# Loading q and k of two token blocks at once in a fused sliding-window attention and MLP kernel

## The chip, the cores and the metric

The kernel runs on one core of one Trainium2 chip. The metric is the time of one execution on the device in microseconds (us), smaller is better. A core has five engines that run their own instruction streams and meet through semaphores: PE (TensorE, matrix multiply and transpose), DVE (VectorE), ACT (ScalarE), POOL (GpSimd) and SP (SyncE, which here only issues transfers). Transfers between the chip's memory and the core are carried by 16 DMA engines, whichever engine issues them.

## The reference, cut to what matters

Eight sequences of 576 tokens pass through attention with 8 heads of 64 and a window of 128 tokens with a bias linear in the distance; the heads are joined to rows of 512, and each row goes through a layer norm and a two-layer MLP (512 to 2048 to 512) with a residual.

```python
scores = scale * np.matmul(q, k.transpose(0, 1, 3, 2))        # q, k, v: [8, 8, 576, 64] f32
mask = (rel >= 0) & (rel < window)                            # window = 128
scores = np.where(mask, scores + bias[None], -1000000000.0)
attn = softmax(scores)                                        # written out in the original
x = np.matmul(attn, v)                                        # then [8, 576, 512]
xn = (x - mu) / np.sqrt(var + 1e-06) * g_ln
out = x + np.maximum(xn @ w_ch1, 0.0) @ w_ch2
```

## The kernel before, in words

**Tiling.** The 8 × 576 = 4608 tokens form 36 blocks of 128. Two sequences are nine blocks (a "pair"); the fifth block of each pair holds the last 64 tokens of one sequence and the first 64 of the next, so its loads are split in two (`where`, L316). A block needs keys and values of itself and of the block before it. For the MLP the blocks are joined to ten chunks of 2, 3, 4, 3, 4, 4, 4, 4, 4, 4 blocks (L229).

**One block of attention** (`attention`, L412). SP loads q, k and v in f32, one token per partition, 8 runs of 64 numbers each (L329). q and k are cast to f16 (L427, `cq` and `ck`), v too (L440, `cv`). For blocks 0 to 11 PE turns q and k with eight 128×128 transposes into one bank of PSUM (L450, task `T`), and one copy of 1024 numbers per partition takes them to the tile `qkt` (L458 or L460, `ev`); for blocks 12 to 35 a transposing DMA does this (L465). PE multiplies q and k (L485, `S`) into a pair of score banks `sc`, of which there is only one set. In blocks 0 to 5 PE first lays the bias into those banks (L500, `Z`), in the others a mask is multiplied in after the exponential (L531, `mka` and `mkb`, one for each half of the heads). ACT takes the exponential (L524), PE multiplies with v (L548), and DVE normalises (L564, L568), takes the statistics (L585, L590) and forms the centred and scaled row `xs` (L596), for which it needs `g_t`, the layer norm's factor spread over all partitions. `xs` is turned by PE (L608, `TX`, with a copy at L616 or L618) for blocks 0 to 13, by a DMA (L623) from there on.

**One chunk of the MLP** (`mlp`, L645): for each of 16 slices of the hidden layer four matmuls (L657, phase A) and a relu (L667 or L669); then for each block 16 matmuls (L683, phase B), the residual (L691) and a store (L699). The weights come in eight transfers that POOL issues and that cast to f16 on the way (L404 for the first matrix, `w0` to `w3`; L406 for the second, `w4` to `w7`). Slice f of phase A needs transfer f // 4. `W_AFTER` (L393) says behind which cast each is issued: 3 × block + 0, 1, 2 for the casts of q, k, v.

**The order of the work.** Nothing is scheduled by the compiler. `Plan.run` (L88) simulates the engines and queues with a duration for each task, takes on each engine the ready task with the smallest value `v`, and gives out every instruction in the order so found; so each engine's order is fixed when the kernel is built, and an engine stands still when the next instruction in its order is not ready. A task of attention has a value that puts it `LEAD` × `SPAN` = 52 us of planned time ahead of the MLP of the same block (L311). A task with several engines in its cost goes where the plan says it ends first; `PICK` (L258) overrides the default engine for single tasks. The plan's transfers share the engines by `rates` (L82): while POOL's queue moves, SP's is planned at 0.17 of full speed. Rings of tiles (L285 to L301) set how far each loader may run ahead: five tiles each of `q32` and `k32`, four of `qk16` and `qkt`.

**Before 26 us of planned time** (`WARM`, L257) PE's planned gaps are filled with matmuls on a tile of zeros (`keep_warm`, L710, L712), which keeps its clock up and computes nothing of the result.

The lines that set the order:

```python
    def av(i, stage=0.0):
        return (i / CB - LEAD) * SPAN + stage
    W_AFTER = [8, 14, 15, 15, 16, 17, 17, 18]
            return {q: 0.92 if q == "DMA POOL" else 0.17 / (len(on) - 1) for q in on}
```

Of the kernel before, what the change touches and what calls it, by code (L numbers as in the profile page):

```python
# [46 lines left out]
class Plan:  # L47
# [6 lines left out]
    QUEUE_ROOM = 4.0  # L54
    LANDING = 2.0

# [18 lines left out]
    def transfer(self, name, eng, issue, secs, room, emit, deps=(), v=0.0):  # L75

        i = self.add(name + ".i", (eng, issue), emit, deps, v, lat=0.0)
        d = self.add(name, ("DMA " + eng, secs), None, [i], v, lat=self.LANDING)
        i.room = d.room = room
        return i, d  # L80

    def rates(self, queues):  # L82
        on = [q for q, x in queues.items() if x]
        if "DMA POOL" in on and len(on) > 1:
            return {q: 0.92 if q == "DMA POOL" else 0.17 / (len(on) - 1) for q in on}
        return {q: 1.0 / len(on) for q in on}

    def run(self):  # L88
# [7 lines left out]
        queues = {e: [] for e in sorted({e for t in self.tasks for e in t.eng if e.startswith("DMA")})}  # L96
        free = dict.fromkeys(engines, 0.0)
        avail = {e: [] for e in engines}
# [6 lines left out]
        for t in self.tasks:  # L105
            if t.left == 0:
                heap.append((0.0, n, t))
                n += 1
# [6 lines left out]
        def done(t):  # L115
            nonlocal n
            for u in t.users:
                u.ready = max(u.ready, t.end + t.lat)
                u.left -= 1
                if u.left == 0:  # L120
                    heapq.heappush(heap, (u.ready, n, u))
                    n += 1
# [7 lines left out]
        while left:  # L130
# [60 lines left out]
            for q in rate:  # L191
                if queues[q][0][1] <= 1e-9:
                    t = queues[q].pop(0)[0]
                    t.end = now
                    used[q] -= t.room
                    self.order.append((t, q, None))
                    left -= 1
                    done(t)
# [5 lines left out]
def kernel(  # L204
# [10 lines left out]
    nc = tc.nc  # L215
# [41 lines left out]
    WARM = 26.0  # L257
    PICK = {('xt', 0): 'ACT DVE', ('xt', 8): 'ACT DVE', ('cv', 5): 'ACT', ('cv', 0): 'POOL ACT', ('ev', 8): 'DVE ACT', ('ev', 1): 'ACT', ('mkb', 8): 'POOL', ('mkb', 3): 'POOL', ('mka', 2): 'DVE', ('mkb', 4): 'POOL'}  # L258
    G_AT = 1.3
    BY_BIAS = 6  # L260
    MASK_AT = 6
    QK_BY_DMA = 12
    X_BY_DMA = 14

    plan = Plan()

    def sb(name, shape, dt):
# [16 lines left out]

    q32 = ring("q32", 5, [P, H, D], FP32)  # L285
    k32 = ring("k32", 5, [P, H, D], FP32)
    v32 = ring("v32", 5, [P, H, D], FP32)
    qk16 = ring("qk16", 4, [P, 2, d_model], FP16)
    vx = ring("vx", 5, [P, H, VD], FP16)
    qkt = ring("qkt", 4, [P, 2, HP, P], FP16)  # L290
    probs = ring("probs", 3, [P, 4, 2, 2 * P], FP16)
# [8 lines left out]
    rstd = ring("rstd", 4, [P, CB], FP32)  # L300
    rec = ring("rec", 4, [P, 4], FP32)  # L301

    scs = [psum.tile([P, 2, 512], FP32, tag=f"sc{n}", name=f"sc{n}") for n in range(2)]
# [20 lines left out]

    def load(name, src, r, i, v):
        got = []
        for p0, n, b, s0 in where(i):
            def emit(e, bank, p0=p0, n=n, b=b, s0=s0):
                nc.sync.dma_start(  # L329
                    out=r[i][p0 : p0 + n, :, :],  # L330
                    in_=src[b, :, s0 : s0 + n, :].rearrange("h p d -> p h d"),
                )
            t, d = plan.transfer(f"{name}{i}", "SP", 0.6, 1.22 * n / P, n / P, emit, (), v)
            r.writes(i, t)
            got.append(d)
        return got

    setup = []
    nc.scalar.preload_act_table_set("natural_log_exp_and_others")
    nc.vector.memset(warm_t, 0.0)  # L340
    nc.vector.memset(eps_t, eps)
    for t in vx.tiles:
        nc.vector.memset(t[:, :, D:VD], 1.0)

    d_iden = plan.transfer("iden", "ACT", 0.5, 0.15, 0.0, lambda e, b: nc.scalar.dma_start(out=iden, in_=iden_dram.ap()), (), -1e6)[1]
    d_dist = plan.transfer("dist", "ACT", 0.5, 0.45, 0.0, lambda e, b: nc.scalar.dma_start(out=dist_t, in_=dist_dram.ap()), (), -9e5)[1]
    d_g = plan.transfer(
        "g", "SP", 0.6, 1.3, 0.12,
        lambda e, b: nc.sync.dma_start(out=g_t, in_=moe_g_ln.unsqueeze(0).broadcast_to([P, d_model])), (), av(G_AT) - 300,  # L349
    )[1]  # L350

# [7 lines left out]
    for bank in range(4):  # L359
        for slot in range(2):  # L360
            def emit(e, b, bank=bank, slot=slot):
                nc.scalar.activation(
                    out=mreg[:, bank, slot, :], in_=dist_t[:, 0, :], func=AF.Exp,
                    scale=-float(slopes[head_of(bank, slot)]),
                )
            tm.append(add(f"mreg{bank}{slot}", ("ACT", 0.4), emit, [d_dist], av(MASK_AT, -10.0)))
    tmix, tnew = [], []
# [15 lines left out]

    loads, kept = {}, {}
    for i in range(NBLK):
        vl = av(i) - 300
        loads[i] = (
            load("q", q, q32, i, vl),
            load("k", k, k32, i, vl + 0.01),
            load("v", v, v32, i, vl + 0.02),  # L390
        )

    W_AFTER = [8, 14, 15, 15, 16, 17, 17, 18]  # L393
    t_w = {}

    def weights(i, casts):

        for n, at in enumerate(W_AFTER):
# [9 lines left out]
            t_w[n] = plan.transfer(f"w{n}", "POOL", 0.8, 3.2, 0.0, emit, [casts[at % 3]] + last, av(i, -60.0))  # L408

    qkt_done, vx_done, aggr_done, xs_done, xt_done = {}, {}, {}, {}, {}  # L410

    def attention(i):  # L412
# [7 lines left out]
        def e_cast(a, src):  # L420
            def emit(e, b):
                en = {"POOL": nc.gpsimd, "DVE": nc.vector}.get(e)
                s = src[i][:, :, :].rearrange("p h d -> p (h d)")
                if en is None:
                    nc.scalar.activation(out=qk16[i][:, a, :], in_=s, func=AF.Copy)
                else:
                    en.tensor_copy(out=qk16[i][:, a, :], in_=s)  # L427
            return emit

        def pick(name, default, **cost):  # L430
            return {e: cost[e] for e in PICK.get((name, i), default).split()}
        cq = add(f"cq{i}", pick("cq", "POOL", POOL=0.62, ACT=0.6, DVE=0.35), e_cast(0, q32), lq, av(i, 0.0))
        ck = add(f"ck{i}", pick("ck", "POOL", POOL=0.62, ACT=0.6, DVE=0.35), e_cast(1, k32), lk, av(i, 0.1))
        q32.reads(i, cq); k32.reads(i, ck); qk16.writes(i, cq); qk16.writes(i, ck)

# [6 lines left out]
        v32.reads(i, cv); vx.writes(i, cv)  # L442
        weights(i, (cq, ck, cv))

        if i < QK_BY_DMA:
            def e_t(e, b):
                pt = fb[b][:, :].bitcast(FP16).rearrange("p (a hp c) -> p a hp c", a=2, hp=HP)
                for a in range(2):
                    for hp in range(HP):
                        nc.tensor.transpose(pt[:, a, hp, :], qk16[i][:, a, hp * P : hp * P + P], iden[:, :])  # L450
            tt = add(f"T{i}", ("PE", 0.48), e_t, [cq, ck, d_iden], av(i, 1.0), acq=("fb", f"T{i}"))
            qk16.reads(i, tt)

            def e_ev(e, b):
                src = fb[plan.held[f"T{i}"][1]][:, :].bitcast(FP16)
                dst = qkt[i][:, :, :, :].rearrange("p a hp c -> p (a hp c)")
                if e == "DVE":
                    nc.vector.tensor_copy(out=dst, in_=src)  # L458
                else:
                    nc.scalar.activation(out=dst, in_=src, func=AF.Copy)  # L460
            ev = add(f"ev{i}", pick("ev", "DVE", DVE=0.7, ACT=1.02), e_ev, [tt], av(i, 1.2), rel=f"T{i}")
            qkt.writes(i, ev)
        else:
            def e_td(e, b):
                nc.sync.dma_start_transpose(  # L465
                    out=qkt[i][:, :, :, :].rearrange("p a hp c -> p (a hp) c"),
                    in_=qk16[i][:, :, :].rearrange("p a d -> p (a d)"),
                )
            ti, ev = plan.transfer(f"QT{i}", "SP", 1.4, 1.4, 1.0, e_td, [cq, ck], av(i, -4.0))
            qk16.reads(i, ev)  # L470
            qkt.writes(i, ti)
        qkt_done[i] = ev

        prev = [] if r == 0 else [qkt_done[i - 1]]

# [32 lines left out]
        if bias:  # L508
            z_ = [add(f"Z{i}", ("PE", 0.87 if r else 0.46), e_z, t_sid + [d_dist], av(i, 1.5), acq=("sc", f"S{i}"))]
        else:  # L510
            z_ = []
        s_ = add(f"S{i}", ("PE", 0.64 if r else 0.42), e_s, z_ + [ev] + prev, av(i, 2.0), acq=("sc", f"S{i}"))
        qkt.reads(i, s_)
# [200 lines left out]
    with tc.manual_schedule():  # L714
        busy = 0.9
        for t, e, b in order:
# [36 lines left out]
```

## Time and profile before

| | us |
|---|---|
| median of 7 executions | 331.96 (330.15 to 333.29) |
| the profiled execution: time | 330.3 |
| its span, from the first to the last event in the trace | 328.5 |
| PE idle between 38.4 and 324.6 us | 2.3 of 286.1 |
| last landing of v's second part for block 4, as its cast shows it | 26.9 |
| first matmul of phase A | 24.9 |

The profile is one execution recorded by the hardware. Its row for an engine and a line gives the number of instructions, their busy time and the mean of one; matmuls overlap, so a busy PE need not be at its peak, and 16 matmuls with 128 columns of output take less than 16 times the duration of one. The chain of waits follows the last instruction back to whatever released it, step by step. A table of windows gives the busy time of every engine in stretches of the span, with the share of time in which the 16 DMA engines held a packet (it passes 1 where packets overlap) and the rate at which bytes moved.

In the first 200 us of 328.5 the DMA engines are busy all the time; 150,704 of the 159,696 packets are under 512 bytes, since a row of one head is 64 × 4 = 256 bytes. The store of an output block moves packets of 2 KB. The granted clock of PE is 0.998 over the span.

### The profile page before, as it was taken

What the parts mean: (1) busy time and instruction counts of PE and PEld (TensorE: products, weight loads), DVE (VectorE), ACT (ScalarE), POOL (GpSimd) and SP (SyncE); (2) the same over time, 40 slices, a digit from 0 to 9 for tenths busy, and PEclk for the clock granted to TensorE, in tenths of its full rate; (3) what the DMA queues carried; (4) which work ended last, traced back from release to release, by engine and by line L of the source; (5) the groups of instructions that cost most, each with busy time, mean ns of one, the idle gap of its engine ahead of it and who ended that gap; (6) DMA issues with size and microseconds to landing.
All of it is one profiled execution on the core that took longest, in us unless ns stands there. A gap on an engine that the chain in (4) does not pass through costs nothing.

```text
span 328.5 us, 6816 instructions
## 1 busy us (share of the span) xinstructions
PE 318.4 (97%) x2701; PEld 175.4 (53%) x2701; DVE 182.6 (56%) x402; ACT 155.0 (47%) x249; POOL 80.8 (25%) x126
## 2 busy tenths in 40 slices
PE   8998899989999999899999999999999999999995
PEld 8987665655544565444554544444455444444442
DVE  1488714799801299844885566656556755511011
ACT  5445554534740582557336722772277227405600
POOL 3848102585300233123322422412000000000000
PEclk9999999999999999999999999999999999999999
DMA  9999999999999999999999999624323220011011
GB/s 184 210 194 193 203 195 210 228 199 235 265 218 219 264 197 165 213 255 213 193 203 228 192 204 261 134 48 116 99 49 76 90 86 21 20 64 64 2 64 64
DMA packets 159696, 52.06 MB, mean 158 GB/s; under 512 B 150704, under 2 KB 154928, under 8 KB 159664
## 3 DMA queue, kind: packets, MB, share of 16 engines
q1 hardware_dynamic: 155152, 47.20, 72.6%
q0 software_dynamic: 4224, 4.19, 7.7%
q8 instruction: 21, 0.34, 0.5%
q10 hardware_dynamic: 288, 0.23, 0.2%
q14 instruction: 11, 0.09, 0.1%
HBM read 37.19 MB, written 9.44 MB: 142 GB/s over the span
## 4 chain that ended last, share of the span: by engine, by line
PE 84%; SPq 6%; DMA 5%; DVE 3%; issue 1%; POOL 0%; ACT 0%; POOLq 0%
PE fb L657 37%; PE fb L683 37%; SPq L329 5%; PE sc L485 5%; PE fb L548 4%; DMA w1sb<-in_moe_w_ch_dram 3%; DMA v<-in_v_dram 2%; PE fb L608 1%; DVE ot L691 1%; DVE xs L596 1%; DVE probs L531 0%; DVE xb L568 0%; PE fb L450 0%; DVE st L585 0%; SPq L349 0%
## 5 line engine op out<-in xcount | busy, mean ns | idle before, releaser
L657 PE MATMUL fb<-xt,w1sb 128*128 128x512 f16 (+2 forms) x640 | 134.0, 358 | 2.1 <-DMA w1sb<-in_moe_w_ch_dram 1.9
L683 PE MATMUL fb<-w2sb,ht 128*128 128x512 f16 x576 | 132.3, 379 | 0.1
L669 ACT ACTIVATE ht<-fb 128x512 f16<-128x512 f32 (+2 forms) x143 | 79.9, 560 | 91.6 <-PE fb L657 89.2
L657 PEld LDWEIGHTS <-w1sb 128*128 128x128 f16 x640 | 59.5, 98 | 57.9 <-DMA w1sb<-in_moe_w_ch_dram 2.5
L524 ACT ACTIVATE probs<-sc 128x1024 f16<-128x1024 f32 (+1 forms) x72 | 67.4, 973 | 44.4 <-PE sc L485 44.3
L683 PEld LDWEIGHTS <-ht 128*128 128x128 f16 x576 | 53.6, 98 | 59.4 <-issue 0.2
L691 DVE SCALAR_TENSOR_TENSOR ot<-fb,rstd,xb 128x512 f32<-128x512 f32 x36 | 26.9, 748 | 60.8 <-PE fb L683 58.2
L531 DVE TENSOR_TENSOR probs<-probs,mreg 128x1024 f16<-128x1024 f16 (+1 forms) x47 | 31.1, 666 | 25.7 <-ACT probs L524 25.5
L440 POOL CAST vx<-v 128x512 f16<-128x512 f32 x34 | 21.4, 634 | 87.3 <-PE fb L548 60.0
L427 POOL CAST qk<-q 128x512 f16<-128x512 f32 x36 | 23.5, 654 | 66.9 <-DMA qkt<-qk 50.1
L568 DVE TENSOR_TENSOR xb<-fb,rec 128x256 f16<-128x256 f32 x72 | 30.0, 421 | 2.1
L548 PEld LDWEIGHTS <-probs 128*128 128x128 f16 x544 | 23.6, 97 | 13.4 <-DVE probs L531 3.4
L596 DVE SCALAR_TENSOR_TENSOR xs<-xb,mv,g_t 128x512 f16<-128x512 f16 x36 | 29.1, 807 | 1.1
L548 PE MATMUL fb<-vx,probs 128*128 128x65 f16 x544 | 26.6, 193 | 1.4 <-DVE probs L531 1.1
L427 POOL CAST qk<-k 128x512 f16<-128x512 f32 x36 | 23.6, 655 | 14.6 <-DMA k<-in_k_dram 6.4
L585 DVE BATCH_NORM_STATS2 st<-xb 128x6 f32<-128x512 f16 x36 | 24.9, 690 | 0.8
L564 DVE RECIPROCAL rec<-fb 128x4 f32<-128x4 f32 x72 | 12.7, 177 | 17.5 <-PE fb L548 17.0
L485 PEld LDWEIGHTS <-qkt 64*128 64x128 f16 x544 | 15.4, 94 | 11.1 <-issue 10.2
L485 PE MATMUL sc<-qkt 64*128 64x128 f16 x288 | 19.4, 216 | 0.0
L485 PE MATMUL sc<-qkt,qkt 64*128 64x128 f16 x256 | 18.1, 219 | 0.4 <-DVE qkt L458 0.3
L712 PE MATMUL fb<-warm_t 128*128 128x128 f16 x197 | 15.8, 241 | 1.0 <-DVE warm_t L340 1.0
L458 DVE COPY qkt<-fb 128x1024 f16<-128x1024 f16 x11 | 7.5, 679 | 13.6 <-PE fb L450 6.9
(35 smaller groups left out, 105.5 us busy)
## 6 DMA issues: line engine op xcount, KB each, us to landing
out_dram<-ot SPq DMA_DIRECT2D x36, 256.0 KB, 2.8
q<-in_q_dram SPq DMA_DIRECT2D x32, 256.0 KB, 5.0
k<-in_k_dram SPq DMA_DIRECT2D x32, 256.0 KB, 4.9
v<-in_v_dram SPq DMA_DIRECT2D x32, 256.0 KB, 4.6
w1sb<-in_moe_w_ch_dram POOLq DMA_DIRECT2D x4, 512.0 KB, 8.0
w2sb<-in_moe_w_ch_dram POOLq DMA_DIRECT2D x4, 512.0 KB, 16.1
q<-in_q_dram SPq DMA_DIRECT2D x8, 128.0 KB, 5.0
k<-in_k_dram SPq DMA_DIRECT2D x8, 128.0 KB, 4.5
```

The source lines that it names most:

```text
L427: en.tensor_copy(out=qk16[i][:, a, :], in_=s)
L485: nc.tensor.matmul(scs[half][:, g, c0 : c0 + P], kt[rows, 1, hp, :], qkt[i][rows, 0, hp, :], start=not bias, stop=True, skip_group_check=True,
L524: nc.scalar.activation(out=o, in_=n_, func=AF.Exp, scale=inv_sqrt_d)
L531: en.tensor_tensor(out=pv, in0=pv, in1=mask[:, 2 * half : 2 * half + 2, :, lo:], op=ALU.mult)
L548: nc.tensor.matmul(pp[:, hh * (D + 1) : hh * (D + 1) + D + 1], probs[i][:, bank, slot, side * P : side * P + P], vx[i - 1 + side][:, h, 0 ...
L568: nc.vector.tensor_tensor(out=xb[i][:, 256 * half : 256 * half + 256].rearrange("p (h d) -> p h d", d=D), in0=pp[:, :, 0:D], in1=rec[2 * i ...
L585: nc.vector.bn_stats(out=st[i][:, :], in_=xb[i][:, :])
L596: nc.vector.scalar_tensor_tensor(out=xs[i][:, :], in0=xb[i][:, :], scalar=mv[c][:, j, 0:1], in1=g_t[:, :], op0=ALU.subtract, op1=ALU.mult,)
L657: nc.tensor.matmul(fb[b][:, 0:n_], w1sb[:, kb, f * P : f * P + P], xt[c][:, kb, 0:n_], start=(kb == 0), stop=(kb == NKB - 1),)
L669: nc.scalar.activation(out=ht[c][:, f, 0:n_], in_=src, func=AF.Relu)
L683: nc.tensor.matmul(pm[:, :], ht[c][:, f, j * P : j * P + P], w2sb[:, f, :], start=(f == 0), stop=(f == NFB - 1),)
L691: nc.vector.scalar_tensor_tensor(out=ot[i][:, :], in0=fb[plan.held[key][1]][:, :], scalar=rstd[c][:, j : j + 1], in1=xb[i][:, :], op0=ALU. ...
```

## The change

**The loads.** In the first pair of sequences, blocks 0 and 1, 2 and 3, 5 and 6, 7 and 8 form four spans of 256 tokens. q and k of a span are loaded in one transfer each, 512 KB, with tokens 2p and 2p+1 on partition p, so that a run is 512 bytes (`load_span`, tiles `qs` and `ks`). Block 4 and the blocks from 9 on load as before. One cast of 1024 numbers per partition for q and one for k puts even tokens before odd ones (`qs16`, `ks16`). PE turns q of both blocks into one bank and k of both into another, eight transposes each; each bank is then copied out in two parts, one for each block, that write every second column, so that the tokens stand in order in `qkt`. v is loaded as before.

**Beside it:** `g_t` is no longer loaded by SP as 128 copies of a row; one row is loaded on ACT's queue and spread by a matmul with a row of ones and a copy (`G`, `Gc`). The distance table comes in two transfers. `W_AFTER` puts w1, w2 and w3 behind the v cast of block 4, w4 behind that of block 5, and w5 to w7 behind that of block 6. PE turns q and k up to block 12 (`QK_BY_DMA` 13) and `xs` up to block 10 (`X_BY_DMA` 11). `q32` and `k32` have four tiles instead of five, `qkt` five instead of four. The plan has other landing times, a later begin, and a reserve of 0.1 us (0.4 us after 30 us of plan, 0.5 us behind POOL's transfers) before PE uses what another engine made. `PICK` is longer: among what it now says, both mask products of block 6 go to POOL (`mka`, `mkb`), that of block 8 goes back from POOL to DVE, and of the two-part copies three are on ACT, one on either.

```diff
@@ class Plan
-    LANDING = 2.0
+    BEGIN = 0.75
+    LANDING = {"DMA SP": (0.7, 1.3), "DMA ACT": (0.7, 1.3), "DMA POOL": (1.6, 1.4)}
+    LAST_OF_RUN = 1.0
...
-            return {q: 0.92 if q == "DMA POOL" else 0.17 / (len(on) - 1) for q in on}
+            a, b = (0.92, 0.17) if len(queues["DMA POOL"]) > 1 else (0.7, 0.4)
+            return {q: a if q == "DMA POOL" else b / (len(on) - 1) for q in on}
...
-                u.ready = max(u.ready, t.end + t.lat)
+                late = self.slack(t, t.end) if "PE" in u.eng and "PE" not in t.eng else 0.0
+                u.ready = max(u.ready, t.end + t.lat + late)
@@ constants
+    SPANS = [0, 2, 5, 7]
+    SLACK = (0.1, 0.4, 0.5)
-    QK_BY_DMA = 12
-    X_BY_DMA = 14
+    QK_BY_DMA = 13
+    X_BY_DMA = 11
-    q32 = ring("q32", 5, [P, H, D], FP32)
-    k32 = ring("k32", 5, [P, H, D], FP32)
+    q32 = ring("q32", 4, [P, H, D], FP32)
+    k32 = ring("k32", 4, [P, H, D], FP32)
-    qkt = ring("qkt", 4, [P, 2, HP, P], FP16)
+    qkt = ring("qkt", 5, [P, 2, HP, P], FP16)
+    qs = ring("qs", 2, [P, H, 2 * D], FP32)
+    ks = ring("ks", 2, [P, H, 2 * D], FP32)
+    qs16 = ring("qs16", 2, [P, 2, H, D], FP16)
+    ks16 = ring("ks16", 2, [P, 2, H, D], FP16)
@@ g
+    d_row = plan.transfer("g", "ACT", 0.5, 0.02, 0.0, lambda e, b: nc.scalar.dma_start(out=g_row[:, :], in_=moe_g_ln.unsqueeze(0)), (), -8e5)[1]
+    def e_g(e, b):
+        nc.tensor.matmul(fb[b][:, :], one_t[:, :], g_row[:, :], start=True, stop=True)
...
+    t_g = add("G", ("PE", 1.3), e_g, [d_row], av(0, 4.0), acq=("fb", "G"))
+    d_g = add("Gc", {"ACT": 0.6, "DVE": 0.69}, e_gc, [t_g], av(0, 4.5), rel="G")
@@ loads
+    def load_span(name, src, r, n, i, v):
+        (_, _, b, s0), = where(i)
+        def emit(e, bank):
+            nc.sync.dma_start(
+                out=r[n][:, :, :],
+                in_=src[b, :, s0 : s0 + 2 * P, :].rearrange("h (p t) d -> p h (t d)", t=2),
+            )
+        t, d = plan.transfer(f"{name}{i}", "SP", 0.6, 1.75, 1.0, emit, (), v)
...
-    W_AFTER = [8, 14, 15, 15, 16, 17, 17, 18]
+    W_AFTER = [8, 14, 14, 14, 17, 18, 18, 20]
...
-        weights(i, (cq, ck, cv))
+        weights(i, (cv, cv, cv) if i in span_of else (cq, ck, cv))
@@ attention, the first block of a span
+                for a, r_, w_ in ((0, qs, qs16), (1, ks, ks16)):
...
+                        dst = w_[n][:, :, :, :]
+                        src = r_[n][:, :, :].rearrange("p h (t d) -> p t h d", t=2)
...
+                    cs = add(f"c{key}", pick(f"cs{a}", "POOL", POOL=1.25, ACT=1.02), e_c, [span_load[n][a]], av(i, 0.1 * a))
...
+                        for hp in range(HP):
+                            for t in range(2):
+                                nc.tensor.transpose(
+                                    pt[:, hp, t, :], w_[n][:, t, 2 * hp : 2 * hp + 2, :].rearrange("p h d -> p (h d)"), iden[:, :]
+                                )
+                    tt = add(key, ("PE", 0.48), e_t, [cs, d_iden], av(i, 1.0 + 0.01 * a), acq=("fb", key))
...
+                    for blk in range(2):
+                            src = fb[plan.held[key][1]][:, :].bitcast(FP16).rearrange("p (hp t c) -> p hp t c", hp=HP, t=2)[
+                                :, :, :, HALF * blk : HALF * blk + HALF
+                            ]
+                            dst = qkt[i + blk][:, a, :, :].rearrange("p hp (c t) -> p hp t c", t=2)
...
+                        ev = add(f"e{key}{blk}", pick(f"ev{a}{blk}", "DVE ACT", DVE=0.6, ACT=0.6), e_ev, [tt], av(i + blk, 1.2), rel=key)
```

## The prediction

> **What bounds the kernel now.** I read the chain of waits first, in order of time:
>
> ```profile
> 19.53 0.74 SPq L329
> 20.32 6.43 DMA v<-in_v_dram
> 26.87 0.61 POOL vx L440
> 27.66 0.50 issue
> 28.17 0.55 POOL qk L427
> 28.72 9.67 DMA w1sb<-in_moe_w_ch_dram
> 38.44 2.57 PE fb L657 x20
> ```
>
> Everything before these lines is SP issuing loads (L329, and L349 for g_t). So the chain is: fifteen loads until v of block 4 has landed, its cast, the q cast of block 5, the weight transfer w2 behind it, and from 38.44 us PE. Then the windows before and after that point, and the groups of PE up to it:
>
> ```profile
> 24.90:38.40 13.50, 11.26 (x160) 8.97 (x160) 11.72 (x32) 7.09 (x12) 6.72 (x10) 1.00 1.22 196
> 38.44:324.56 286.12, 283.85 (x2176) 144.79 (x2176) 158.22 (x330) 136.06 (x217) 59.87 (x92) 1.00 0.77 154
> L712 PE MATMUL fb<-warm_t 128*128 128x128 f16 x197 | 15.8, 241 | 1.0 <-DVE warm_t L340 1.0
> ```
>
> Second and third number of a window: its length, and PE's busy time. After 38.44 PE idles 2.3 of 286 us: there it is the bound, and little can be won. Before it, PE runs 197 matmuls on zeros, about 0.06 us apart (a run of 20 spans 1.12 us of weight loads), so 11.8 us, and idles 2.2 us in the second window. This is what an earlier supply can turn into work: when the loads and weights come x us sooner, PE is saturated x us sooner and the rest follows. That the first 38 us wait for bytes and not for an engine is in the last two columns of the windows (DMA share, GB/s):
>
> ```profile
> 10.00:15.00 5.00, 5.00 (x93) 4.48 (x87) 3.13 (x8) 2.16 (x4) 3.70 (x7) 1.00 1.19 215
> 60.00:80.00 20.00, 18.96 (x205) 11.16 (x203) 17.93 (x39) 9.81 (x15) 13.54 (x17) 1.00 1.20 205
> 298.00:324.00 26.00, 26.00 (x122) 11.79 (x121) 1.80 (x3) 9.35 (x16) 0.00 (x0) 1.00 0.10 36
> ```
>
> **Loads.** Between 10 and 15 us there are only 256-byte packets: 215 GB/s over 16 engines is 13.4 GB/s each, 19 ns a packet, 1.22 us for a 256 KB load (64 packets per engine). No 512-byte packet exists in this trace. The near row on the other side is the 2 KB packet of the stores: 26 us × 16 × 0.10 = 41.6 us of engine time for 36 GB/s × 26 us = 0.94 MB, 457 packets, 91 ns each. On the line between the two, 512 bytes take 19 + 256 × 72 / 1792 = 29 ns, so a span load takes 64 × 29 ns = 1.88 us where two loads took 2.44: 0.56 us less. The ends: 1.22 us (a packet costs the same whatever its size) and 2.44 us (bytes alone count). A rule speaks for less: the Trainium skill, DMA: Bandwidth & Descriptors, section "Why small descriptors are slow (HBM only)", charges a packet its 32-byte beats plus 3 cycles, 11 for 256 bytes and 19 for 512, so 2.44 × 19/22 = 2.11 us, 0.33 less. I take the line between the rows, because the rule gives a 2 KB packet 67 beats, 6.1 times a small one, and the rows say 91/19 = 4.8. Up to v of block 4 there are four span loads: **−2.3 us** by the rows, −1.3 by the rule, 0 to −4.9 by the ends. The four span loads after it come behind that point and are not counted.
>
> g_t was 128 packets of 2 KB on the same queue ahead of block 2's loads: 8 per engine × 91 ns, **−0.7 us**. Its substitute is hidden: one matmul in place of zeros, one copy of about 0.7 us while DVE is busy 1.84 of the first 10 us; g_t is first read at 13.4 us, and a row on ACT's idle queue lands in about 2 us, as iden did (1.9). Uncovered it would cost that copy. The later two thirds of the distance table are wanted only by block 4, and their 0.5 us issue stands before no exponential that is late.
>
> **Weights.** w1 was issued at 27.43, w2 at 28.72, since block 5's q cast lay between; an issue takes 0.75. Back to back, w2 gains **−0.5 us**, and the loads of block 5 no longer come before it. Sum for w2's landing: 38.44 − 3.5 = 34.9. What is late next? Z, S and the exponentials share one set of score banks: 22.22 (Z of block 3) to 25.68 (its exponentials' end), 3.8 us a block with the hand-over. With block 0 at about 10.3 (one longer load and cast: its q landed at 3.96 and k at 5.77, now some 0.7 and 1.3 later), S of block 4 can be at 25, where it was at 29.39; so these banks do not bind. Block 5's span, two loads of 512 KB, now queues behind w1 to w3 and comes at some 38 to 41 us where S of block 5 ran at 33.04. Its 2.4 us of PE work move back; phase A of chunks 0 and 1, for which w0 to w3 are there, covers it.
>
> **PE's own work.** Transposes of q and k: eight per block as before, plus block 12: +0.45 us (the chain has eight L450 at 0.45); three blocks' TX fewer, 4 each, 0.22 us: −0.66. **−0.2 us.** DVE loses three copies of 0.42 and gains one of 0.68. One DMA transpose of q and k goes, three of xs come; SP's queue is far from the end there.
>
> **Copies out of PSUM.**
>
> ```profile
> L458 DVE COPY qkt<-fb 128x1024 f16<-128x1024 f16 x11 | 7.5, 679 | 13.6 <-PE fb L450 6.9 <-ACT ht L669 6.7
> L616 DVE COPY xt<-fb 128x512 f16<-128x512 f16 x12 | 5.1, 422 | 5.5 <-PE fb L608 5.4
> L531 POOL TENSOR_TENSOR probs<-probs,mreg 128x1024 f16<-128x1024 f16 x1 | 2.5, 2487 | 1.8 <-ACT probs L524 1.8
> 68.27 1.95 DVE L596 SCALAR_TENSOR_TENSOR xs<-xb,mv,g_t 128x512 f16<-128x512 f16 x1
> ```
>
> The first two rows: 512 more numbers cost 257 ns,[...] over 165 ns of fixed cost. The new copies write every second number. Here a rule speaks against the change: the Trainium skill, VectorE: DVE Perf Modes, section "Mode 2×_1P", asks for a step of one for two f16 per cycle. By the rows at full rate a half copy costs 0.42, by the rule 0.165 + 512 × 1.04 ns = 0.70 us. I take 0.70. Of 16 half copies three are on ACT and one on either, where the nearest row (L618, 512 numbers) is 0.59; 12.5 on DVE are 8.8 us against 4.8 for seven whole ones, so +4 us of DVE (+0.4 at full rate), half of it before 25 us and half at 40 to 60. The cover: DVE is busy 6.9 of 20 us at 40 to 60, but 18.1 of 22 at 18 to 40. **+0.5 us**, between 0 and 2 if none of the first half is covered. The casts of 1024 on POOL are two of 0.61 in one, no loss but the wait for the whole.
>
> **Masks.** The third and fourth row: a mask product takes 2.49 us on POOL, where the plan counts 1.4; while it ran (67.17 to 69.66), xs on DVE took 1.95 instead of 0.75, and PE idled 1.0 us for it (the 60 to 80 window). This one returns to DVE: **−1.0 us**. Both of block 6 go to POOL: their second half ends 2 × 1.09 = 2.2 us after plan, less the 0.4 of reserve, 1.8. PE's order is fixed and L548 of block 6 stands before MLP matmuls that are ready. How many stand between is not in the trace, so half: **+0.9 us**, from 0 to what rival D says.
>
> **Sum:** −2.3 − 0.7 − 0.5 − 0.2 − 1.0 + 0.5 + 0.9 = −3.3 us. The profiled execution took 330.3 (span 328.5 and 1.8 around it): 327.0. It lies 1.7 below the median of the runs shown; moved to that, 331.96 − 3.3 = **328.7 us**. About 0.5% (1.7 us) is what a measurement of this kernel tells from no change.
>
> **Rivals.**
> - **C, packets cost the same whatever their size.** Then four span loads save 4.9 instead of 2.3: 326.1. For it: DMA share above 1 with small packets, so something other than the bytes fills the engines. Against: 2 KB packets do take longer.
> - **B, the transfer is hidden anyway.** Bytes bind, or the weight transfers, spaced by their own bytes (phase A goes on at 33.60 with w1 and at 38.44 with w2, 4.8 us apart), bind from w0 on. The span loads give nothing: 328.7 + 2.3 = 331.0. For it: 6.4 us from issue to landing of w0 beside the loads. Against: w1 itself waits for block 4's v.
> - **D, POOL's masks of block 6 become the bound.** Two of 2.49 us one behind the other, and DVE held behind each, by 1.2 us as seen or by all of 2.49; mean 1.85. With 2.2 us after plan: 2.2 + 2 × 1.85 = 5.9 in place of 0.9: **333.7**. It decides the sign from 4.2 us of standstill at block 6 (3.3 + 0.9). For it: the 1.0 us that one such product already cost. Against: at 40 to 60 DVE has room and PE has phase A and B of two chunks.
>
> **Chances.** Forecast 0.50 (327.2 to 330.2: the ends of copies, weights and the rule for the loads), C 0.18, B 0.16, D 0.16. The range takes in C with half a microsecond and B, and of D the lighter part: 325.6 to 332.8. Faster by over 0.5% (below 330.3): forecast, C and a little of B, 0.69. Slower by over 0.5% (above 333.6): D from its middle on, and what I may have missed in a new fixed order of every engine, 0.15. Within: 0.16.
>
> **What would show it.** Loads: span loads 1.9 us apart while they follow each other, over 240 GB/s before 15 us; v of block 4 cast near 24 instead of 26.87. Weights: first L657 near 22.5 instead of 24.89, the last wait for a weight at 35. Fewer L712, by about 50. Copies: half copies on DVE at 0.70. Masks: L531 on POOL twice at 2.5 and an idle PE before L548 of block 6. The prediction is wrong if v of block 4 lands no earlier, or if PE's idle time after its saturation grows from 2.3 us to over 5.

## The result, and the profile after

The changed kernel takes **327.5 us** (median of 12 executions, 326.6 to 329.9) where the kernel before takes 332.2. The medians differ by 4.6 us; the ratio over all executions, which is used from here on, is 0.9873, 95% interval 0.9848 to 0.9898, so 4.2 us less, between 3.4 and 5.0. The forecast was 3.3 us less. Executions more than 1.5% above the fastest of their kernel are left out of every ratio as slow: ten of 22 for the kernel without spans, its profiled one among them, and at most three for any other. The profiled execution took 327.1 (span 325.3), 3.2 us under that of the kernel before.

The chain of waits of the changed kernel, in order of time (start, length, what):

```profile
9.44 7.90 DMA v<-in_v_dram
...
20.25 10.76 DMA v<-in_v_dram
...
32.49 6.77 issue
39.31 2.12 POOL probs L636
...
42.20 2.14 POOL probs L636
...
44.39 0.42 PE fb L653 x8
44.81 2.39 PE fb L762 x16
```

It no longer ends its first part in a wait for a weight. It runs through two v loads, through 6.8 us in which POOL had nothing to do (it waited for ACT's exponentials), and from 39.3 us through the mask products of block 6 on POOL (lines have moved: L762 is phase A, L788 phase B, L653 the product with v, L636 the mask, L817 the matmuls on zeros).

Windows of the changed kernel (columns: length, then busy time of PE, PEld, DVE, ACT, POOL, granted clock, DMA share, GB/s):

```profile
5.00:10.00 5.00, 5.00 (x61) 4.03 (x59) 0.69 (x1) 4.17 (x11) 2.84 (x4) 1.00 1.23 260
10.00:15.00 5.00, 4.94 (x88) 4.47 (x87) 1.02 (x4) 3.96 (x8) 4.35 (x5) 1.00 1.17 250
15.00:20.00 5.00, 4.39 (x89) 3.89 (x83) 3.93 (x10) 3.85 (x6) 3.22 (x5) 1.00 0.74 161
20.00:30.00 10.00, 7.57 (x133) 6.61 (x127) 7.21 (x16) 5.33 (x8) 7.29 (x10) 1.00 1.15 226
30.00:40.00 10.00, 10.00 (x156) 8.72 (x154) 8.65 (x24) 9.12 (x17) 1.99 (x3) 1.00 1.20 223
40.00:60.00 20.00, 19.45 (x167) 11.56 (x165) 9.65 (x19) 12.37 (x24) 11.04 (x11) 1.00 1.15 219
60.00:80.00 20.00, 20.00 (x185) 11.28 (x184) 17.04 (x40) 7.75 (x13) 9.63 (x15) 1.00 1.04 231
80.00:140.00 60.00, 60.00 (x496) 31.94 (x494) 36.82 (x76) 30.27 (x49) 13.97 (x22) 1.00 1.15 209
```

The same for the stretches before and after 40 us, first of the kernel before, then of the changed one, and the zeros of the changed one (columns of the last line: busy time, mean ns of one, idle time before them):

```profile
0.00:40.00 40.00, 36.13 (x540) 31.98 (x541) 24.23 (x72) 19.79 (x35) 21.81 (x36) 1.00 1.16 197
40.00:140.00 100.00, 97.76 (x851) 54.38 (x849) 61.11 (x130) 48.67 (x81) 32.28 (x48) 1.00 1.16 217
```

```profile
0.00:40.00 40.00, 35.90 (x543) 31.73 (x544) 22.77 (x69) 27.72 (x46) 19.90 (x29) 1.00 1.06 217
40.00:140.00 100.00, 99.45 (x845) 54.78 (x842) 63.51 (x134) 50.39 (x85) 34.63 (x47) 1.00 1.13 215
L817 PE MATMUL fb<-warm_t 128*128 128x128 f16 x176 | 13.9, 244 | 1.0 <-DVE warm_t L363 1.0
```

**Where the time came from.** Over the whole span PE's busy time falls from 318.4 to 316.6 us and its idle time from 10.1 to 8.7. The 21 matmuls on zeros that are gone make some 1.3 us of the busy time (0.06 us each). The idle time has moved: before 40 us it is 4.1 us where it was 3.9, from 40 to 140 it is 0.55 where it was 2.2, and after 140 it is the same 4.0. So PE is full from 30 us on, not from 38.4; but 1.7 of the 3.2 us between the two profiles come from idle time after 40 us, where the prediction saw little to win. PE is not fed as predicted either. The timeline of POOL and PE in the changed kernel:

```profile
18.45 0.88 POOL L466 DMA_DIRECT2D w1sb<-in_moe_w_ch_dram  x1
21.36 0.61 POOL L504 CAST vx<-v 128x512 f16<-128x512 f32 x1
22.80 0.75 POOL L466 DMA_DIRECT2D w1sb<-in_moe_w_ch_dram  x1
26.13 1.27 POOL L520 CAST qs<-qs 128x1024 f16<-128x1024 f32 x1 [2.58 <-DMA qs<-in_q_dram]
27.35 1.48 POOL L466 DMA_DIRECT2D w1sb<-in_moe_w_ch_dram  x2
...
27.46 0.62 PE L530 MATMUL fb<-iden,qs 128*128 128x128 f16 x8 [1.59 <-POOL qs L520]
...
30.57 1.92 PE L762 MATMUL fb<-xt,w1sb 128*128 128x256 f16 x16
```

v of block 4 is cast at 21.36 us where it was 26.87, and w1 is issued at 22.80 where it was 27.43. That is 5.5 us, and the prediction had 2.9 (near 24). The two loads of this v now go out ahead of the first weight transfer, w0, at 18.45; in the kernel before they went out behind it. First the kernel before, then the changed one:

```profile
18.42 0.93 POOL L404 DMA_DIRECT2D w1sb<-in_moe_w_ch_dram  x1
19.53 1.62 SPq L329 DMA_DIRECT2D v<-in_v_dram  x2
```

```profile
16.41 1.31 SPq L352 DMA_DIRECT2D v<-in_v_dram  x2
```

The second of the two took 6.4 us from its issue to its landing before (20.32 to 26.75) and takes 3.7 now (17.09 to 20.79). The other profiles agree: issued 0.6 us or more ahead of w0 it took 3.7 to 5.0 us, issued less than 0.2 us ahead or behind 5.5 to 7.5.

But w2 and w3 wait in POOL's queue behind the cast of the span of block 5, whose load is late, until 27.35 (before: 28.72). The plan of the change lets 1.6 us pass between one weight's issue and the next (the first number of `LANDING` for POOL), and that let the cast in between. Phase A begins at 30.57, *later* than the 24.89 of before; what has moved ahead is attention: scores of block 6 start at 37.8 us instead of 50.1.

### The profile page after: what moved, and what is told of

The parts are those of the page before. It is cut to its first block, busy times and chain, and to the rows that moved or that the text cites. A ratio compares the mean times of both kernels' runs of the same rounds, so it can differ in the third digit from the quotient of the medians.

```text
span 325.3 us, 6755 instructions
## 1 busy us (share of the span) xinstructions
PE 316.6 (97%) x2678; PEld 174.1 (54%) x2678; DVE 185.0 (57%) x402; ACT 162.0 (50%) x259; POOL 81.0 (25%) x116
## 3 DMA queue, kind: packets, MB, share of 16 engines
q0 software_dynamic: 4224, 4.19, 7.8%
## 4 chain that ended last, share of the span: by engine, by line
PE 85%; DMA 6%; POOL 3%; SPq 3%; issue 2%; DVE 0%; ACT 0%; POOLq 0%
PE fb L788 38%; PE fb L762 36%; DMA v<-in_v_dram 6%; PE sc L590 5%; PE fb L653 4%; POOL probs L636 1%; SPq L352 1%; SPq L428 1%; PE fb L555 1%; POOL vx L504 0%; POOL w2sb L468 0%; PE fb L713 0%; PE fb L530 0%; POOL w1sb L466 0%; ACT qkt L544 0%
## 5 line engine op out<-in xcount | busy, mean ns | idle before, releaser
L762 PE MATMUL fb<-xt,w1sb 128*128 128x512 f16 (+2 forms) x640 | 134.9, 358 | 0.1
L788 PE MATMUL fb<-w2sb,ht 128*128 128x512 f16 x576 | 133.2, 379 | 0.0
L774 ACT ACTIVATE ht<-fb 128x512 f16<-128x512 f32 (+2 forms) x138 | 77.2, 562 | 92.4 <-PE fb L762 90.9
L762 PEld LDWEIGHTS <-w1sb 128*128 128x128 f16 x640 | 59.3, 98 | 55.9 <-issue 0.5
L788 PEld LDWEIGHTS <-ht 128*128 128x128 f16 x576 | 53.4, 98 | 59.4
L796 DVE SCALAR_TENSOR_TENSOR ot<-fb,rstd,xb 128x512 f32<-128x512 f32 x36 | 26.9, 748 | 56.1 <-PE fb L788 55.7
L636 DVE TENSOR_TENSOR probs<-probs,mreg 128x1024 f16<-128x1024 f16 (+1 forms) x46 | 30.6, 671 | 19.5 <-ACT probs L629 19.4
L653 PEld LDWEIGHTS <-probs 128*128 128x128 f16 x544 | 24.2, 97 | 12.2 <-POOL probs L636 0.7
L490 POOL CAST qk<-q 128x512 f16<-128x512 f32 x28 | 19.0, 679 | 40.3 <-DMA qkt<-qk 17.2
L669 DVE RECIPROCAL rec<-fb 128x4 f32<-128x4 f32 x72 | 12.3, 175 | 28.3 <-PE fb L653 28.1
L653 PE MATMUL fb<-vx,probs 128*128 128x65 f16 x544 | 26.7, 193 | 0.7 <-POOL probs L636 0.4
L690 DVE BATCH_NORM_STATS2 st<-xb 128x6 f32<-128x512 f16 x36 | 24.9, 690 | 0.9
L490 POOL CAST qk<-k 128x512 f16<-128x512 f32 x28 | 19.6, 702 | 7.7 <-DMA k<-in_k_dram 5.6
L772 DVE TENSOR_SCALAR ht<-fb 128x512 f16<-128x512 f32 (+2 forms) x22 | 12.6, 577 | 6.2 <-PE fb L762 5.6
L817 PE MATMUL fb<-warm_t 128*128 128x128 f16 x176 | 13.9, 244 | 1.0 <-DVE warm_t L363 1.0
```

Of the source, the lines that this page charges most:

```text
L490: en.tensor_copy(out=qk16[nrm[i]][:, a, :], in_=s)
L636: en.tensor_tensor(out=pv, in0=pv, in1=mask[:, 2 * half : 2 * half + 2, :, lo:], op=ALU.mult)
L653: nc.tensor.matmul(pp[:, hh * (D + 1) : hh * (D + 1) + D + 1], probs[i][:, bank, slot, side * P : side * P + P], vx[i - 1 + side][:, h, 0 ...
L690: nc.vector.bn_stats(out=st[i][:, :], in_=xb[i][:, :])
L762: nc.tensor.matmul(fb[b][:, 0:n_], w1sb[:, kb, f * P : f * P + P], xt[c][:, kb, 0:n_], start=(kb == 0), stop=(kb == NKB - 1),)
L774: nc.scalar.activation(out=ht[c][:, f, 0:n_], in_=src, func=AF.Relu)
```

## The experiments

Each kernel was timed against the kernel before on the same chip; the ratios below are to it, with 95% intervals, and 0.001 is 0.33 us. Two kernels are compared with each other through their ratios.

**The size of the runs.** The span load's access is changed and nothing else; PE's order is the same.

```diff
-                out=r[n][:, :, :],
-                in_=src[b, :, s0 : s0 + 2 * P, :].rearrange("h (p t) d -> p h (t d)", t=2),
+                out=r[n][:, :, :].rearrange("p h (t d) -> p (h t) d", t=2),
+                in_=src[b : b + 2, :, s0 : s0 + P, :].rearrange("b h p d -> p (b h) d"),
```

> The changed kernel with every instruction in the same order on every engine; only the span loads move the same 512 KB in runs of 256 bytes (16 heads of two sequences, one token per partition, in place of 8 heads and two tokens), so what q and k hold for these blocks is other data and the output is not the reference's. Supply theory (the prediction's): each of the four span loads ahead of v of block 4 costs 0.56 us more, v of block 4 is cast 2.3 us later than in the changed kernel (21.4 us), and the time rises by 2.0 to 2.5 us over the changed kernel (about 329.8). Order theory (the gain comes from the new fixed order and its reserve, which removes PE's idle time after 60 us): PE's order is the same here, so the time rises by less than 0.8 us.

Measured: 0.9936 [0.9914, 0.9958], 2.1 us above the changed kernel (±1.1 from the two intervals). POOL's timeline in this kernel:

```profile
24.03 0.60 POOL L504 CAST vx<-v 128x512 f16<-128x512 f32 x1
25.47 0.75 POOL L466 DMA_DIRECT2D w1sb<-in_moe_w_ch_dram  x1
28.23 1.04 POOL L520 CAST qs<-qs 128x1024 f16<-128x1024 f32 x1 [2.01 <-DMA qs<-in_q_dram]
29.20 1.48 POOL L466 DMA_DIRECT2D w1sb<-in_moe_w_ch_dram  x2
```

v of block 4 is cast 2.67 us later. It landed 2.4 us later (23.21 against 20.79; the cast also waits for POOL's other work): four span loads, 0.6 each. In this profile PE idles 6.0 us before 30 us instead of 4.1, and nothing from 60 to 140, as in the changed kernel. So everything else in the change, with small runs, brings about half of the gain (2.1 of 4.2 us), the supply theory holds for the runs, and PE's idle time after 60 us goes with the new order, whatever the size of the runs. The order pays for it with idle time before 40 us, and the larger runs take that away again.

**The step of two in the copies.** Two loads of 128 tokens each, and a copy per block without gaps:

```diff
...
-                                :, :, :, HALF * blk : HALF * blk + HALF
+                                :, :, blk, :
                             ]
-                            dst = qkt[i + blk][:, a, :, :].rearrange("p hp (c t) -> p hp t c", t=2)
+                            dst = qkt[i + blk][:, a, :, :]
```

> The changed kernel with the same plan, but each span load as two loads of 128 tokens with runs of 256 bytes into the two halves of the tile, so that the copies out of PSUM write a block's columns without gaps; the output is the reference's. Against the kernel with small runs alone this gives the price of the copies with a step of two. If the step costs DVE its second number per cycle, a half copy on DVE falls from 0.73 to about 0.42 us and the time falls by up to 0.5 us against that kernel; if the price of a half copy is not on PE's path, no change between the two (within 0.3).

Measured: 0.9938 [0.9913, 0.9962], the same as with the step. The copies themselves did get cheaper. One row for each engine, from the changed kernel (step of two) and then from this one (no step), min/median/max in ns:

```profile
L542 DVE COPY qkt<-fb x5: 730/733/741, 15.7 to 55.5; 128x512 f16<-128x512 f16 x5
L544 ACT ACTIVATE qkt<-fb x11: 731/742/755, 9.3 to 54.7; 128x512 f16<-128x512 f16 x11
```

```profile
L543 DVE COPY qkt<-fb x5: 423/424/425, 16.7 to 59.4; 128x512 f16<-128x512 f16 x5
L545 ACT ACTIVATE qkt<-fb x11: 591/597/598, 9.3 to 58.8; 128x512 f16<-128x512 f16 x11
```

So the step costs 0.31 us a copy on DVE and 0.15 on ACT, 5 × 0.31 + 11 × 0.15 = 3.2 us of the two engines in all, and none of it is seen in the time. This kernel also makes two transfers of each span load, so the two effects could offset each other; the two ratios tell a difference from about 1 us on.

**No spans, all else kept** (`SPANS = []`).

> The changed kernel with no spans at all: q and k of all blocks loaded block by block as before, everything else of the change kept (plan's timing model and reserve, row of g, weights' places, engines chosen). The plan makes another order from it. Supply theory: the 2.3 us of loads come back and the time is 329.5 to 330.5. Order theory: at most 328.3, with little idle time of PE after 60 us.

Measured: 1.0023 [0.9993, 1.0052]: 5.0 us above the changed kernel and no better than before. That is more than the loads' runs cost in the same order. In its profile v of block 4 goes out behind w0 again (19.93 against 16.23) and is cast at 26.86, as in the kernel before, though g no longer stands in the queue. The engines and weight places that the change names were chosen for an order with spans; how much that adds was not tried.

**The plan's waits for weights taken away** (`LAST_OF_RUN = 0.0`, third number of `SLACK` 0.0).

> The changed kernel with the plan's extra waits for weight transfers taken away (1.0 us after the last one of a run, 0.5 us of reserve). In the changed kernel the first matmul of phase A stands at 30.6 us, though its weights were issued at 18.5 and took 6.4 us before the change; PE idles 1.6 us at 26 us meanwhile. If the plan's pessimism about weights holds phase A back and that costs time: first phase A near 27 to 28, less idle time between 20 and 30 us, 0.5 to 1.5 us faster. If PE's work is conserved and only swapped, or PE then waits for weights that are not there: no change or up to 1 us slower.

Measured: 0.9892 [0.9849, 0.9934], not told from the changed kernel, and phase A began at 32.8 us, not earlier. The new order put other work first; the question is left to the weights' kernel below.

**The mask product that leaves POOL, on the kernel before.**

```diff
-                en = nc.vector if e == "DVE" else nc.gpsimd
+                en = nc.vector if e == "DVE" or i == 8 else nc.gpsimd
```

> The kernel before with PE's order untouched; only the one mask product that ran on POOL (second half of block 8, 2.49 us) is made by DVE at its place, as in the changed kernel. The prediction's term: xs on DVE no longer takes 1.95 us there, PE's 1.0 us of idle time behind it goes, 1.0 us faster than before (about 331.2). Rival: DVE is busy 18 of 20 us there, so 0.7 us more of it makes another wait, within 0.3 us of before.

Measured: 1.0021 [1.0006, 1.0036], 0.7 us *slower*, against 1.0 faster in the prediction. PE still waits for `xs` in this kernel's profile. The numbers are us in all, times, and the longest; before they were 1.2, 2 and 1.0:

```profile
PE fb L608 <- DVE xs L596: 1.9, 4, 0.9
```

At block 8 PE stands 0.46 us for the copy of `qkt` and 0.51 for `xs`, 0.97 together, where it stood 0.98 for `xs`: DVE, busy 18 of 20 us at 60 to 80, is late by as much elsewhere. Why the whole is 0.7 us slower is not shown; this profile's extra idle time lies before 40 us (6.3 us against 3.9), ahead of the edit.

**The timing model alone, on the kernel before** (landing times, begin, reserve and rates of the change; nothing else of it).

> The kernel before with the changed kernel's timing model alone (landing times, begin, reserve of 0.1 and 0.4 us before PE uses another engine's result, 0.5 us behind weights): no spans, g and weights and engines chosen as before. Order theory, for the part of the gain that the size of the runs does not give: PE's idle time after 60 us falls from about 2.1 to under 0.5 us and the time by 1.0 to 2.0 us. Rival: the model alone gives nothing (within 0.7 us of before) or, since engines were chosen for another plan, is slower.

Measured: 1.0135 [1.0083, 1.0187], 4.5 us slower. In its profile PE idles 1.35 us from 60 to 80 and 2.1 from 80 to 140, more than before. So neither the model nor the reserve brings the gain by itself; that the whole new order takes away the idle time after 60 us stands, since the kernel with small runs shows it.

**The two mask products of block 6 on DVE, on the changed kernel** (as in the last diff, with `i == 6`).

> The changed kernel with PE's order untouched; the two mask products of block 6 (2.12 us each on POOL, not the 2.49 that was predicted) are made by DVE at their places. The prediction's term of +0.9 us for them: the chain that ended last goes through both and through PE's wait behind them, so 0.4 (the idle time that PE shows there) to 0.9 us faster than the changed kernel. Rival: DVE takes the work over where its own steps are late and gives it back, no change within 0.3 us.

Measured: 0.9897 [0.9867, 0.9927], not faster than the changed kernel. The chain of waits leads through these products, yet taking them off POOL wins nothing that six executions can show.

**g on SP's queue again, on the changed kernel.**

```diff
+                if name == "v" and i == 1:
+                    nc.sync.dma_start(out=ot[0][:, :], in_=moe_g_ln.unsqueeze(0).broadcast_to([P, d_model]))
```

> The changed kernel with every order untouched and one transfer more: the 128 copies of the row g, 2 KB each, are loaded again on SP's queue behind v of block 1, into a tile that nobody reads yet. The prediction's term: 0.7 us of the queue, v of block 4 cast 0.7 us later than 21.4, the time up by 0.5 to 0.9 us. Rival: the queue has 0.7 us to spare between 15 and 20 us, where the DMA share falls to 0.74 in the changed kernel, and nothing is late: within 0.2 us.

Measured: 0.9955 [0.9936, 0.9973], 2.7 us (±1.0) above the changed kernel: as much as all four span loads' runs. The transfer lands in a tile that nobody reads yet. SP's queue in this kernel, and the cast of v of block 4:

```profile
5.08 2.06 SPq L357 DMA_DIRECT2D ot<-in_moe_g_ln_dram  x1
7.18 0.43 SPq L430 DMA_DIRECT2D qs<-in_q_dram  x1
...
17.52 1.31 SPq L352 DMA_DIRECT2D v<-in_v_dram  x2
...
18.17 0.88 POOL L468 DMA_DIRECT2D w1sb<-in_moe_w_ch_dram  x1
...
24.80 0.61 POOL L506 CAST vx<-v 128x512 f16<-128x512 f32 x1 [2.51 <-DMA v<-in_v_dram]
```

The next load is issued at 7.18 instead of 4.94 us, and v of block 4 is cast 3.4 us later than in the changed kernel. w0, in POOL's own queue, is issued at 18.17, about as before (18.45). The second load of this v goes out at 18.20, 1.1 us later than in the changed kernel and now level with w0, and takes 6.5 us to land where it took 3.7. So 1.1 us in the queue became 3.9 at the landing.

**A bridge over PE's idle time.** In that profile PE idled 2.3 us at 26 to 28 us, and the granted clock (third column from the end) then fell:

```profile
26.00:28.00 2.00, 0.10 (x2) 0.00 (x0) 0.74 (x1) 0.64 (x1) 1.67 (x3) 1.00 1.25 274
28.00:29.00 1.00, 0.59 (x6) 0.60 (x7) 0.00 (x0) 0.00 (x0) 1.00 (x2) 0.71 1.00 166
29.00:30.00 1.00, 1.00 (x17) 1.00 (x15) 0.52 (x1) 0.00 (x0) 1.00 (x3) 0.50 1.08 180
...
32.00:33.00 1.00, 1.00 (x27) 0.82 (x24) 0.61 (x2) 0.40 (x1) 0.04 (x1) 1.00 1.27 241
```

The edit, put once on the changed kernel and once on the kernel with g:

```diff
+                        if key == "T5.0":
+                            for _ in range(20):
+                                nc.tensor.matmul(fb[b][:, 0:P], warm_t[:, :], warm_t[:, :], start=True, stop=True)
```

> The changed kernel with 20 matmuls on zeros (1.2 us) ahead of the first transposes of the span of blocks 5 and 6, where PE idles 1.6 us for the cast of q in the profile of the changed kernel. Where that idle time reached 2.3, 3.0 and 3.5 us in other runs, PE's granted clock fell to 0.5 for some 3 us behind it; after 1.6 and 1.7 it did not. Seven executions of the changed kernel lie at 326.6 to 327.6 us, five at 328.3 to 329.9. Clock theory: the upper group is that drop, met when the load is late; with the gap bridged it goes, all executions at 326.6 to 328, the median 0.3 to 0.8 us under the changed kernel's. Rival (the two groups have another cause, or the filler delays the transposes): the upper group stays, the median the same or up to 1 us slower.

> The changed kernel with the 128 copies of g on SP's queue again, and the same 20 matmuls on zeros ahead of the first transposes of blocks 5 and 6. Without the filler this kernel took 2.7 us more than the changed one: v of block 4 was cast 3.4 us later, PE idled 2.3 us at 28 us and its clock stood at 0.5 for 3 us. Clock theory: the clock's part is about 1.6 us and goes, so 1.0 to 1.8 us faster than with g and no filler (near 0.990 of the kernel before). Rival, the queue's part is all: no change (0.9955).

Measured: 0.9867 [0.9832, 0.9902] and 0.9971 [0.9943, 0.9999]. Neither is faster than the same kernel without the bridge. On the changed kernel the upper group stayed: three of six executions at a mean clock of 0.993 or 0.994 and 328.0 to 329.8 us, three at 1.000 and 326.7 to 327.2. With g, half of the executions now ran at 0.997 or more (without the bridge 3 of 21), and the median did not fall. But the six at 0.997 or more have a median of 330.5 us, where those of the changed kernel have 327.1: with the clock up, g still costs. So the clock's drop is at most a part of what g cost. For the changed kernel the question stays open: the profile of the kernel of block 6's masks, with the same order up to there, shows an idle gap of 3.48 us in this place, which 1.2 us of zeros do not fill.

**Weights one behind the other, on the changed kernel** (`"DMA POOL": (0.0, 2.0)`, `LAST_OF_RUN = 0.0`, third number of `SLACK` 0.0).

> The changed kernel with the plan's timing of weight transfers as it was before the change (no wait from one issue to the next, landing after 2.0 us, no reserve). POOL's order then has w1, w2 and w3 one behind the other before the cast of the span of block 5, where w2 and w3 came 3.8 us later behind that cast. Supply theory, as the prediction took it (w2's landing decides): w2 and w3 some 3 us earlier, first phase A near 25 us, 1 us or more faster than the changed kernel. Rival: loads and weights share the DMA engines, the span of block 5 comes later by what the weights gain, PE waits for it longer and its clock falls; 1 to 3 us slower.

Measured: 0.9904 [0.9865, 0.9943], not told from the changed kernel. w1, w2 and w3 did go out from 22.9 us on, before the cast of the span:

```profile
22.90 2.23 POOL L466 DMA_DIRECT2D w1sb<-in_moe_w_ch_dram  x3
25.11 1.07 POOL L520 CAST qs<-qs 128x1024 f16<-128x1024 f32 x1
31.64 1.04 POOL L520 CAST ks<-ks 128x1024 f16<-128x1024 f32 x1 [5.45 <-PE fb L530]
...
28.09 1.05 PE L762 MATMUL fb<-xt,w1sb 128*128 128x256 f16 x8 [2.40 <-DMA w1sb<-in_moe_w_ch_dram]
...
26.00:28.00 2.00, 0.00 (x0) 0.00 (x0) 1.25 (x3) 0.00 (x0) 0.18 (x1) 1.00 1.23 261
28.00:29.00 1.00, 0.91 (x9) 0.82 (x10) 0.00 (x0) 0.26 (x1) 0.00 (x0) 1.00 1.24 215
```

Phase A came at 28.1 instead of 30.6, but PE waited 2.4 us for a weight, w0. Issued 3.7 us earlier, w2 landed only 1.2 us earlier (35.1 against 36.4); w0 landed 3.3 us later (28.1 against 24.7) and k of block 5 3.6 us later (31.5 against 27.9). What the later weights gain, w0 and the loads lose. The last two lines are windows: here the clock stayed at 1.00 after the wait.

**No g on SP's queue, on the kernel before** (the transfer left out, `g_t` set to ones, so this kernel leaves out the layer norm's factor).

> The kernel before with every order untouched, without the 128 copies of g on SP's queue: g_t is set to ones on POOL at the start, so the layer norm's factor is left out. The prediction's term: 0.7 us faster than before. If the load of g costs what it did in the changed kernel's order (2.2 us of SP's queue, from the issue of the next load): 1.5 to 2.7 us faster.

Measured: 0.9956 [0.9935, 0.9977], 1.5 us faster than before (0.8 to 2.2). v of block 4 is cast at 26.92 us here, no earlier than before: w0 goes out at 17.44 instead of 18.42, still ahead of this v (19.33). w2 too lets PE go on when it did before (38.45 against 38.44). The two profiled executions differ by only 0.1 us (330.2 against 330.3), so the profile does not show where the 1.5 us of the others are won.

## Why the prediction was right, and where its steps were not

The sum was right in sign and nearly in size (3.3 us forecast, 4.2 measured), and its two terms of supply, loads and g, are the two that the runs confirm. The path it gave them, by w2's landing, was not the one taken, and part of the agreement is luck: weights (−0.5) and copies (+0.5) both came to nothing and cancel, and so do the two masks, while g was priced too low. Step by step:

- **Loads, −2.3: right.** Runs of 256 bytes in the same order cost 2.1 us more, ±1.1. That puts rival B, with nothing won by the runs, out, and rival C (4.9 us from them) too, but it does not tell 2.3 from the 1.3 of the rule. The landing of v of block 4 and the packets do. It lands 2.4 us later, which makes a span load 2.44 − 0.6 = 1.84 us, 29 ns a packet, as taken from the line between the 256-byte and the 2 KB row. And from 2 to 16 us of the changed kernel's trace a 512-byte packet took 32.0 ns and a 256-byte one 22.4, so one large takes 0.71 of two small (packets overlap, so these are not shares of the time). The stretch from 10 to 15 us, from which the 19 ns came, does not hold small packets only, as the prediction has it: 74 of g's fall in it. But in the kernel before without g, 4224 small packets go through in 5 us (5 to 10), which is 19 ns each per engine again. The beats of the Trainium skill (DMA: Bandwidth & Descriptors, "Why small descriptors are slow (HBM only)") gave 2.11 us, 0.86; here the measurement decides against it.
- **g, −0.7: mis-sized.** The term was priced as eight 2 KB packets per engine at 91 ns, the row of the stores. In the trace of the kernel before, the 128 packets of g took 147 ns each, 8 × 147 = 1.2 us, and the next load in SP's queue starts 1.2 us later for them (7.81 against 6.59); in the changed order it starts 2.2 us later. Why a row that all 128 copies read takes longer than a store of the same size was not tried. Putting g on the changed kernel cost 2.7 us (1.7 to 3.7); v of block 4 then came level with w0. Taking it from the kernel before won 1.5 us (0.8 to 2.2), by a path that the profile does not show.
- **v of block 4, "near 24": 21.36.** The sum of loads and g gave 3 us and the cast moved by 5.5, and its loads got ahead of w0, which the prediction had not looked at. In every profile the time to land goes with that; moving w0 alone was not tried. It cuts both ways: without spans, and in the kernel before without g, the same v still came behind w0 and was cast at 26.9.
- **Weights, −0.5, and "w2's landing at 34.9 saturates PE": wrong.** w2 left POOL only at 27.35, behind a cast that stood before it in POOL's queue, and landed at 36.4; no weight was waited for; and sending the three weights earlier won nothing. Block 5's span, which the prediction put behind these weights at 38 to 41 us, went out before them and landed at 26.0 and 27.9; so PE was full from 30 us with attention first, and phase A began at 30.6, not near 22.5.
- **"After 38.44 little can be won": wrong.** 1.7 us of PE's idle time between 40 and 140 us are gone, and 0.6 of 291 us are left from 30 us on. It goes with small runs too, so it belongs to the new order, and the front of the kernel pays for it with idle time of its own when the loads are slow. The zeros were 50 fewer in the forecast, 21 in the profile. (The 2.2 us that the prediction puts in "the second window" are those from 24.9 to 38.4 us, the first of its two lines.)
- **Copies, +0.5: price right, cover wrong.** 0.73 us on DVE against the 0.70 taken; but only 5 of 16 went to DVE. The reading of the code was at fault: the default for these copies is `"DVE ACT"`, either engine, not DVE. ACT's cost 0.74 instead of 0.59, and all of it was hidden as far as 1 us can be told.
- **Masks, −1.0 and +0.9: not borne out.** PE's idle time at 60 to 80 us is gone in the changed kernel, but block 8's product on DVE did not do it: alone, it left the kernel before with the same wait there and 0.7 us slower. Block 6's products on DVE made the changed kernel no faster. Rival D is out: PE stands 0.39 us before L653 of block 6, not 4.2. Each product took 2.12 us there.
- **PE's own work, −0.2,** was not tested alone.

Loads (2.1) and g (1.5 to 2.7) together cover 3.6 to 4.8 of the 4.2 us. That everything else adds up to nothing is only what is left over, with about 1 us of error on each, and it is not shown: the parts do not simply add. With the spans taken out the rest of the change, g's row included, gave 1.0023, and its timing model alone 1.0135. No kernel that was run is told from the changed one on the fast side.

## What to carry to other kernels

When the DMA engines feed the first stage of a kernel and its rows are 256 bytes, two tokens per partition can be worth the copies that put them in order: here the data came 2.4 us sooner, the time fell by about as much, and the copies' price was hidden where the copying engines had room. Price every transfer in a queue by when the *next* one starts, a broadcast of one row above all, and not by its bytes; then look at which load it pushes behind a large transfer of another queue, because there 1 us can become 4. A wait that the chain shows, or an idle gap that seems to have one owner, may give nothing when removed; in a fixed order test each on both kernels before counting it.

## What the runs showed of the hardware that was not expected

- **An idle gap of PE of 2.2 to 3.5 us can halve its clock, but its length alone does not decide.** After 2.18, 2.25, 2.30, 2.96 and 3.48 us of idle time in five profiles the granted clock stood at 0.5 for 3.4 to 6.8 us; after 2.32 (no spans) and 2.40 (weights one behind the other) it stayed at 1.00. After single gaps of 1.8 us or less it did not fall. The Trainium skill, TensorE: Matmul & The Clock Gate, "HAM oscillation", warns of gaps over 3.4 us; here shorter ones were enough in four of these places.
- **Executions of one kernel with a mean clock under 0.997 are slower:** the changed kernel 329.2 us (median of four) against 327.1 (of eight), the kernel before 332.9 (39) against 331.5 (79).
- **128 copies of one 2 KB row are slower to read than 2 KB rows are to store:** 147 and 144 ns a packet in two traces, against 86 and 86 for the stores after 200 us of the same traces.
- **A step of two costs ACT as well as DVE:** 742 against 597 ns for 512 f16 out of PSUM.
- **One cast of 1024 on POOL took 1.04 us** at its fastest, where two of 512 took 1.22.
